# The first MLP product in twenty block products per quad, summed in two PSUM banks in five phases

## The chip, the cores and the metric

The kernel runs on one core of a Trainium2 chip. Times are device microseconds of one execution. Three runs of the kernel before took 558.06, 559.64 and 561.53 us; their median, 559.64 us, is the time before.

## The reference

A gated linear attention feeds a two-layer MLP with an ELU between. Inputs of the attention are q, k, v and f_logit with shape (4, 8, 768, 48): batch, heads, tokens, head dimension. w_in is 384 x 2048, w_out 2048 x 384.

```python
f = 1.0 / (1.0 + np.exp(-f_logit))
for t in range(S):
    state = f[:, :, t, :, None] * state + np.einsum('bhd,bhe->bhde', k[:, :, t], v[:, :, t])
    y[:, :, t] = np.einsum('bhd,bhde->bhe', q[:, :, t], state)
x = y.transpose(0, 2, 1, 3).reshape(3072, 384)
h = x @ w_in
g = np.where(h > 0.0, h, np.exp(np.minimum(h, 0.0)) - 1.0)
out = g @ w_out
```

Everything is fp32 in effect. The weights come as 64-bit floats; the kernel splits their words into fp32 itself, in a staging tile `area`, parts of which later hold sums of weight blocks.

## The kernel before

The 3072 tokens are cut into 12 **units** of 256 tokens (u or m = 0 to 11, three to a batch). Of each unit the attention gives x, held in tile `xt` as 128-row blocks: three blocks of rows (the 384 features) by two blocks of 128 tokens. The MLP of a unit runs over eight **pairs** j, each of 256 columns of w_in (two 128-column blocks). Below, p0 to p7 are a unit's pairs. For a pair the work is, in order:

1. *First product* (`up`, `up7`): x times the pair's columns into PSUM tiles `psH`. In units 1 to 11 it isn't done as 12 block products but as 11, with a bilinear scheme: `mix` forms four sums of weight blocks once for each pair, `blend` five differences of x blocks for each unit (on GpSimd), ten instructions (nine 128 wide, one 256 wide) multiply, and `u1`, `hh`, `u43h` on ScalarE and VectorE recombine the results to h (L911, L913, L926).
2. *Exponential* (`exped`): two ScalarE instructions, Relu of -h and Exp, into tile `gg` (L936, L937).
3. *ELU* (`elu`): one VectorE instruction forms g (L958), then four GpSimd instructions form the `sums` of g's blocks (L968).
4. *Second product* (`down`): seven products 192 wide into four PSUM tiles `psM` (L1015). The first and second read g alone, the third reads the third GpSimd sum. At a unit's end five VectorE adds join the four banks (L1025) and DMAs store the rows.

The order is written by hand, and every engine works through its own queue in that order. The main loop counts half-steps T, two to a pair: at even T the first product of pair P = T // 2 is issued, at odd T `joined(P)` and the second product of pair P - 2. A table `plan` puts attention work of later units at half-steps: `gates` (two ScalarE instructions on f, L617, L619), `decays` (a scan and a reciprocal on VectorE, scalings on GpSimd), `transposed`, `both` (state products, scores, the causal mask on VectorE at L722, the state updates at L695), `outputs` and `carried`, whose result ScalarE copies into `xt` (L779, L781); two SyncE DMAs (L784) then fill the gap rows of x, and `blend` may start. `reread` and `check` test the range of the weights, two VectorE reductions each.

The two PSUM banks of the first product have one tag, `h`, with two buffers: each pair takes both in turn. An instruction that waits on ScalarE, VectorE or GpSimd holds back all that stands behind it in that engine's queue.

## Time and profile before

| what | value |
|---|---|
| median of three runs | 559.64 us |
| span of the profiled execution | 557.7 us |
| TensorE (PE) busy | 543.0 us, 97% |
| VectorE (DVE) busy | 406.4 us, 73% |
| GpSimd (POOL) busy | 287.8 us, 52% |
| ScalarE (ACT) busy | 228.3 us, 41% |
| granted TensorE clock, mean | 0.994 |
| first product, 128 wide (PE, L904) | 1584 records in two groups |
| second product (PE, L1015) | 1236 records in four groups |

The page gives the profiled execution's span, from its first to its last instruction; no other time of that execution is listed, so sums are made against 557.7 us. A row of instruction groups has line, engine, operation, tiles out<-in, shapes and count, then the busy time and the mean of one in ns, then the engine's idle time before them and what ended it. An fp32 matrix product of one instruction appears as two records. Records on TensorE overlap, so the mean of one is its latency, not its share of the time. A timeline row has start, duration, engine, line and operation. A row of the chain of waits has start, duration and what ran.

### The profile page before, as it was taken

What the parts mean: (1) busy time and instruction counts of PE and PEld (TensorE: products, weight loads), DVE (VectorE), ACT (ScalarE), POOL (GpSimd) and SP (SyncE); (2) the same over time, 40 slices, a digit from 0 to 9 for tenths busy, and PEclk for the clock granted to TensorE, in tenths of its full rate; (3) what the DMA queues carried; (4) which work ended last, traced back from release to release, by engine and by line L of the source; (5) the groups of instructions that cost most, each with busy time, mean ns of one, the idle gap of its engine ahead of it and who ended that gap; (6) DMA issues with size and microseconds to landing.
All of it is one profiled execution on the core that took longest, in us unless ns stands there. A gap on an engine that the chain in (4) does not pass through costs nothing.

```text
span 557.7 us, 15617 instructions
## 1 busy us (share of the span) xinstructions
PE 543.0 (97%) x6358; PEld 507.9 (91%) x6358; DVE 406.4 (73%) x804; ACT 228.3 (41%) x443; POOL 287.8 (52%) x559
## 2 busy tenths in 40 slices
PE   7889999999999999999999999999999999999996
PEld 3477679999999999999999999999999999999996
DVE  8799888887676776786785785786686687745553
ACT  3279764333434343333434334343343344333331
POOL 6600786475473474375465366357258258325332
PEclk9899999999999999999999999999999999999998
DMA  8998971033035135216217207307307302301001
GB/s 211 261 264 214 278 184 43 4 84 88 3 82 146 30 76 149 63 34 186 68 22 186 81 9 192 87 8 192 86 9 191 88 9 72 88 5 33 31 2 35
DMA packets 39474, 54.30 MB, mean 97 GB/s; under 512 B 4032, under 2 KB 29216, under 8 KB 39392
## 3 DMA queue, kind: packets, MB, share of 16 engines
q1 hardware_dynamic: 38592, 52.61, 36.5%
q8 instruction: 52, 0.85, 0.6%
q10 hardware_dynamic: 800, 0.59, 0.4%
q14 instruction: 30, 0.25, 0.2%
HBM read 45.02 MB, written 4.72 MB: 89 GB/s over the span
## 4 chain that ended last, share of the span: by engine, by line
PE 91%; DMA 2%; DVE 2%; ACT 1%; POOL 1%; issue 1%; SPq 1%; ACTq 0%; DVEq 0%; POOLq 0%
PE psH L904 39%; PE psM L1015 37%; PE psM L981 3%; PE psH L949 2%; PE psY L752 2%; PE psY L772 2%; PE psU_a L737 2%; PE psS L714 2%; PE psT L674 1%; DMA area<-in_moe_w_out_dram 1%; DMA f<-f 1%; ACT area L578 1%; DVE f L636 1%; POOL q L626 1%; DMA f<-in_f_logit_dram 0%
## 5 line engine op out<-in xcount | busy, mean ns | idle before, releaser
L904 PE MATMUL psH<-xt,wi 128*128 128x128 f32 (+1 forms) x1056 | 195.0, 294 | 0.0
L968 POOL TENSOR_TENSOR sums<-gg 128x128 f32<-128x128 f32 x172 | 75.6, 460 | 207.8 <-DVE gg L958 188.1
L936 ACT ACTIVATE gg<-hh 128x512 f32<-128x512 f32 x88 | 55.5, 630 | 249.3 <-DVE hh L926 111.7
L904 PEld LDWEIGHTS psH<-xt,wi 128*128 128x128 f32 x1056 | 149.5, 192 | 1.6
L904 PE MATMUL psH<-xt,area 128*128 128x128 f32 x704 | 121.5, 275 | 0.0
L904 PEld LDWEIGHTS psH<-xt,area 128*128 128x128 f32 x704 | 106.5, 192 | 4.5
L913 DVE TENSOR_TENSOR hh<-psH,u 128x256 f32<-128x256 f32 x88 | 36.9, 419 | 97.8 <-ACT u L911 97.7
L1015 PE MATMUL psM<-area,sums 128*128 128x192 f32 x516 | 99.9, 326 | 0.0
L1015 PEld LDWEIGHTS psM<-area,sums 128*128 128x128 f32 x516 | 86.0, 190 | 0.3 <-issue 0.2
L1015 PE MATMUL psM<-wo,gg 128*128 128x192 f32 x376 | 77.7, 332 | 0.0
L958 DVE SCALAR_TENSOR_TENSOR gg<-gg,hh 128x512 f32<-128x512 f32 x88 | 63.8, 725 | 1.5 <-ACT gg L937 1.5
L636 DVE RECIPROCAL f<-f 128x256 f32<-128x256 f32 x36 | 62.7, 1747 | 1.3
L937 ACT ACTIVATE gg<-gg 128x512 f32<-128x512 f32 x96 | 60.6, 631 | 3.0
L1015 PEld LDWEIGHTS psM<-wo,gg 128*128 128x128 f32 x376 | 60.2, 190 | 1.3
L926 DVE TENSOR_TENSOR hh<-psH,u43h 128x256 f32<-128x256 f32 (+1 forms) x176 | 54.6, 352 | 3.0
L626 POOL TENSOR_TENSOR q<-q,f 128x256 f32<-128x256 f32 x48 | 39.6, 826 | 19.5 <-DMA f<-f 12.9
L968 POOL TENSOR_TENSOR sums<-gg,sums 128x128 f32<-128x128 f32 x86 | 45.4, 528 | 6.7
L626 POOL TENSOR_TENSOR k<-k,f 128x256 f32<-128x256 f32 x48 | 39.3, 821 | 10.2 <-DMA f<-f 8.3
L926 DVE TENSOR_TENSOR u43h<-psH,hh 128x256 f32<-128x256 f32 x88 | 37.0, 420 | 9.2 <-PE psH L904 8.7
L968 POOL TENSOR_TENSOR sums<-sums,gg 128x128 f32<-128x128 f32 x86 | 43.0, 500 | 0.0
L1015 PE MATMUL psM<-area,gg 128*128 128x192 f32 x172 | 42.0, 326 | 0.0
L1015 PE MATMUL psM<-wo,sums 128*128 128x192 f32 x172 | 42.0, 326 | 0.0
(102 smaller groups left out, 646.3 us busy)
## 6 DMA issues: line engine op xcount, KB each, us to landing
area<-in_moe_w_out_dram SPq DMA_DIRECT2D x8, 768.0 KB, 10.6
again<-in_moe_w_in_dram SPq DMA_DIRECT2D x16, 384.0 KB, 3.6
again<-in_moe_w_out_dram SPq DMA_DIRECT2D x16, 384.0 KB, 3.6
k<-in_k_dram SPq DMA_DIRECT2D x12, 384.0 KB, 4.5
q<-in_q_dram SPq DMA_DIRECT2D x12, 384.0 KB, 5.6
v<-in_v_dram SPq DMA_DIRECT2D x12, 384.0 KB, 5.8
area<-in_moe_w_in_dram SPq DMA_DIRECT2D x8, 576.0 KB, 8.3
out_dram<-o SPq DMA_DIRECT2D x42, 96.0 KB, 2.4
```

The source lines that it names most:

```text
L626: e.tensor_tensor(out=t[n][:, p], in0=t[n][:, p], in1=t["f"][:, p, "kq".index(n)], op=ALU.mult)
L636: nc.vector.reciprocal(f[:, p, 1], f[:, p, 0])
L714: nc.tensor.matmul(pc[r][FULL[b], w, p], lhsT=t["k"][FULL[r], p, cols], rhs=t["q"][FULL[r], p, cols], start=True, stop=True,)
L904: nc.tensor.matmul(to, lhsT=lhs, rhs=rhs, start=(n == 0), stop=True, skip_group_check=True)
L913: add = lambda to, x, y: nc.vector.tensor_tensor(out=to, in0=x, in1=y, op=ALU.add)
L926: add = lambda to, x, y: nc.vector.tensor_tensor(out=to, in0=x, in1=y, op=ALU.add)
L936: nc.scalar.activation(g[:], h, AF.Relu, scale=-1.0)
L937: nc.scalar.activation(g[:], g[:], AF.Exp, scale=-1.0)
L958: nc.vector.scalar_tensor_tensor(out=g[:], in0=g[:], scalar=-1.0, in1=phs.pop(P), op0=ALU.add, op1=ALU.max)
L968: nc.gpsimd.tensor_tensor(out=s[:, i], in0=x, in1=y, op=op)
L981: nc.tensor.matmul(pm[t][:], lhsT=g[:, i, t * 128 : (t + 1) * 128], rhs=wo[:, 2 * j + i, :], start=(j == 0 and i == 0), stop=(j == NP - 1 ...
L1015: nc.tensor.matmul(pm[bank][:, half * DH : (half + 1) * DH], lhsT=x, rhs=y, start=first, stop=(j == NP - 1), skip_group_check=True,)
```

## The change

Units 0 and 1 now do their first product plainly: `up` with six instructions, 256 wide, for a pair. From unit 2 on the eight pairs are taken as four **quads** of 512 columns (q0 to q3; quad n has pairs 2n and 2n + 1). A quad's 24 block products become 20, all 128 wide. For this 19 sums of weight blocks are formed once for each two quads in one instruction (`w_sums`, some of them in place of w_in's own blocks, which only the plain units needed), and 12 differences of x blocks for each unit (`blend`; `xt` now has 16 blocks and two buffers).

The 20 products are issued in five **phases** of 3, 5, 5, 4 and 3 (`phase`). Phases 0, 2 and 4 write one PSUM bank, 1 and 3 the other; later phases add to what the bank holds, and after each phase ScalarE copies the running sums to a tile `vals` in SBUF, so that each partial sum is caught on its way. After phase 1 ScalarE also writes one block back to PSUM (`SEED`). After phase 3 four VectorE instructions, after phase 4 three more (`JOIN3`, `JOIN4`, both operands in SBUF) complete h in `vals`.

The main loop from unit 2 on counts steps s, ten to a unit, each with two phases. In a step stand: the `elu` due, the plan's work, two phases with their copies and joins, more of the plan's work, then a number of second products from one running stream (`CHUNKS`: 6, 6, 6, 0, 7, 6, 6, 6, 7, 6), and at the end the exponential steps due: of a quad's first pair in the step where its phase 4 ran, of its second pair in the next. The elu of a pair stands at the start of the following step. The attention steps move with it: A3 places `transposed` in step 1, `both` in step 3, `outputs` in step 5, `carried` in step 6, BL `blend` in step 7; `gates` for the unit after next stands in step 5, its `decays` in steps 5, 7 and 8.

```diff
-    A3 = (2, 5, 9, 11)
-    BL = 13
-    MX = 10
+    D4 = (-9, -6, -4, -1)
+    A3 = (3, 7, 11, 13)
+    BL = 15
-    BL1 = 13
     LIMIT = 2.0**80
...
+        (10, 2, 0, -1), (7, 8, 14, -1), (2, 13, 5, -1), (11, 10, 9, -1), (15, 0, 14, -1), (6, 4, 15, -1),
+    )
...
+        (18, 17, 5, -1), (19, 18, 11, -1), (20, 9, 16, 1), (18, 18, 4, -1), (9, 15, 9, -1), (6, 10, 9, -1),
+        (8, 13, 3, -1), (0, 4, 8, -1), (5, 9, 12, -1), (3, 8, 12, -1), (12, 4, 19, -1), (4, 16, 11, -1),
...
+    PHASES = (
+        (0, 3, 0, 3, ((0, 15, 16), (1, 14, 13), (2, 13, 12))),
+        (1, 14, 0, 4, ((0, 5, 4), (3, 3, 6), (1, 5, 14), (1, 1, 7), (2, 0, 15))),
+        (0, 6, 0, 4, ((0, 12, 20), (1, 7, 8), (2, 4, 18), (3, 10, 1), (3, 4, 2))),
+        (1, 10, 0, 4, ((0, 2, 19), (3, 1, 5), (1, 8, 0), (2, 11, 9))),
+        (0, 0, 1, 3, ((1, 6, 17), (2, 9, 11), (3, 10, 3))),
+    )
+    SEED = (1, 5)
...
+    JOIN4 = (
...
+    PLACES = ((14, ((1, 1), (1, 0), (0, 0), (0, 1))), (4, ((1, 1), (0, 1), (1, 0), (0, 0))))
+    USUAL = ((0, 0), (0, 1), (1, 0), (1, 1))
...
+    def w_block(q, n):
+        if n >= 12:
+            return extra[:, q, n - 12]
+        i, k = divmod(n, NKT)
+        i = (0, 2, 3, 1)[i]
+        return wis[:, q, i // 2, k, i % 2]
+
+    def w_sums(e, q, some):
+        for to, a, b, sign in W_SUMS[some]:
+            e.tensor_tensor(
+                out=w_block(q, to), in0=w_block(q, a), in1=w_block(q, b), op=ALU.add if sign > 0 else ALU.subtract
+            )
 
     order = [divmod(i, NP) for i in range(NU * NP)]
...
+    def x_tile(u):
+        xts[u] = sb.tile([128, 16, 128], FP32, tag="xt", name=f"xt{u}", bufs=2)
+        return xts[u][:, 0:8].rearrange("n (k t) f -> n k (t f)", t=2)
+
...
-    def mix(j):
-
-        a = [[wi[j][:, k, i * 128 : (i + 1) * 128] for k in range(2)] for i in range(2)]
-        t = [mixes[:, j, i] for i in range(4)]
-        for to, x, y, op in (
-            (t[0], a[1][0], a[1][1], ALU.add), (t[1], t[0], a[0][0], ALU.subtract),
-            (t[2], a[0][0], a[1][0], ALU.subtract), (t[3], a[0][1], t[1], ALU.subtract),
-        ):
...
-    def blend(u):
-
-
-        x = xts[u][:].rearrange("n k (t i) -> n (k t) i", t=2)
-        for to, a, b in ((7, 3, 1), (1, 1, 0), (8, 3, 1), (9, 2, 8), (6, 4, 5)):
-            nc.gpsimd.tensor_tensor(out=x[:, to], in0=x[:, a], in1=x[:, b], op=ALU.subtract)
-
...
+    def blend(u, e, some=slice(None)):
+
+        x = xts[u]
+        for to, a, b, _ in X_SUMS[some]:
+            e.tensor_tensor(out=x[:, to], in0=x[:, a], in1=x[:, b], op=ALU.subtract)
+
+    quads = {}
+
+    def joins(n, todo):
+        v = vals[n % 2]
+        pick = lambda a, b: v[:, a : b + 1 : b - a] if b > a else v[:, a : a + 1].broadcast_to([128, 2, 128])
+        for op, to, x, y in todo:
+            nc.vector.tensor_tensor(out=pick(*to), in0=pick(*x), in1=pick(*y), op=op)
+
+    def phase(n, i):
+
+        m, q = PLAIN_UP + n // NQ, n % NQ
+        side, at, frm, size, todo = PHASES[i]
+        if i < 2:
+            quads[n, side] = ps.tile([128, 4, 128], FP32, tag=f"h{(n + side) % 2}", name=f"psH{m}_{q}_{side}")
+        bank = quads[n, side]
+        for t, (slot, x, w) in enumerate(todo):
+            nc.tensor.matmul(
+                bank[:, slot], lhsT=w_block(q, w), rhs=xts[m][:, x], start=(i < 2 and t == 0), stop=True,
+                skip_group_check=True,
+            )
+        v = vals[n % 2]
+        nc.scalar.copy(v[:, at : at + size], bank[:, frm : frm + size])
+        if i == 1:
...
-    def joined(P):
-        m, j = order[P]
-        h, pb = phs[P]
-        add = lambda to, x, y: nc.vector.tensor_tensor(out=to, in0=x, in1=y, op=ALU.add)
-        u43 = sb.tile([128, 2, 128], FP32, tag="u43h", name=f"u43h{m}_{j}")
-        add(u43[:], pb[:, 0::2], h[:, 0:1].broadcast_to([128, 2, 128]))
-        add(h[:, 2:4], pb[:, 1::2], u43[:])
-        add(h[:, 4], pb[:, 0], u43[:, 1])
-        exped(P, h[:, 1:].rearrange("n (i t) f -> n i (t f)", i=2))
-
...
-        if m >= DIRECT:
-            up7(P)
-            return
...
@@ -1009,9 +1041,11 @@
                 todo = todo[3:] + todo[:3]
             starts = ((0, 0), (3, 0), (1, 0), (2, 1)) if j == 0 else ((0, 0), (1, 0)) if j == plain else ()
         started = set()
-        for bank, half, x, y in todo:
+        for n, (bank, half, x, y) in enumerate(todo):
             first = (bank, half) in starts and bank not in started
             started.add(bank)
+            if n:
+                yield
             nc.tensor.matmul(
                 pm[bank][:, half * DH : (half + 1) * DH], lhsT=x, rhs=y,
...
+    for n in range(EARLY):
+        at_step(12 + n, lambda n=n: w_sums(nc.gpsimd, slice(0, 2), slice(n, n + 1)))
+        at_step(22 + n, lambda n=n: w_sums(nc.vector, slice(2, 4), slice(n, n + 1)))
+    for n in range(EARLY, len(W_SUMS)):
+        at_step(26 + (n - EARLY) // 2, lambda n=n: w_sums(nc.vector, slice(0, 2), slice(n, n + 1)))
+        at_step(32 + n - EARLY, lambda n=n: w_sums(nc.gpsimd, slice(2, 4), slice(n, n + 1)))
+    at_step(BL2, lambda: blend(2, nc.vector, slice(0, 6)), lambda: blend(2, nc.gpsimd, slice(6, 12)))
     for u in range(3, NU):
-        t = (u - 1) * NFT
-        at_step(t + BL, lambda u=u: blend(u))
-        at_step(t - 16, lambda u=u: load(u))
-        at_step(t - 8, lambda u=u: gates(u))
-        attention(u, [t + i for i in D3], [t + i for i in A3])
-    joint = [(u - 1) * NFT + A3[1] for u in range(3, NU)]
+        t = base(u - 1)
+        at_step(t + BL, lambda u=u: blend(u, nc.gpsimd))
+        at_step(base(u - 2), lambda u=u: load(u))
+        at_step(t - (8 if u == 3 else 10), lambda u=u: gates(u))
+        attention(u, [t + i for i in (D3 if u == 3 else D4)], [t + i for i in A3])
...
+    for T in range(PLAIN_UP * NFT):
         P = T // 2
...
+    def products():
+        for P in range(PLAIN_UP * NP - LAG, NU * NP):
+            for _ in down(P):
+                yield
+            yield
+
...
+    CHUNKS = (6, 6, 6, 0, 7, 6, 6, 6, 7, 6)
+
+    def exp_pair(n, i):
+        frm, where = PLACES[i]
+        exped(PLAIN_UP * NP + 2 * n + i, vals[n % 2][:, frm : frm + 4], where)
...
+    elu(PLAIN_UP * NP - 1)
+    total = (NU - PLAIN_UP) * NQ
+    for s in range(5 * total // 2):
+        T = PLAIN_UP * NFT + 2 * s
+        for f in elus.pop(s, ()):
+            f()
+        for f in plan.pop(T, ()):
+            f()
+        for i in (2 * s, 2 * s + 1):
+            n, i = divmod(i, 5)
+            phase(n, i)
+            if i == 3:
+                joins(n, JOIN3)
+            elif i == 4:
+                joins(n, JOIN4)
+                for z in range(2):
+                    exps.setdefault(s + z, []).append((n, z))
+        for f in plan.pop(T + 1, ()):
+            f()
+        take((5, 5, 4)[s] if s < 3 else CHUNKS[s % 10])
+        for n, z in exps.pop(s, ()):
+            exp_pair(n, z)
+            elus.setdefault(s + 1, []).append(lambda n=n, z=z: elu(PLAIN_UP * NP + 2 * n + z))
...
+    take(NP * 7)
```

Names in the next rows: `sums7_4` and `gg7_4` belong to unit 7, pair 4; `xt8` is x of unit 8. GpSimd in the second half of unit 7, before:

```order
L626 TENSOR_TENSOR k1_73<-k1_73,f1_71 128x256
L626 TENSOR_TENSOR q1_72<-q1_72,f1_71 128x256
L968 TENSOR_TENSOR sums7_5_4327<-gg7_5_4264 128x128 x2
L968 TENSOR_TENSOR sums7_5_4327<-sums7_5_4327,gg7_5_4264 128x128
L968 TENSOR_TENSOR sums7_5_4327<-gg7_5_4264,sums7_5_4327 128x128
L892 TENSOR_TENSOR xt8_4299<-xt8_4299 128x128 x5
L626 TENSOR_TENSOR k1_73<-k1_73,f1_71 128x256
L626 TENSOR_TENSOR q1_72<-q1_72,f1_71 128x256
L968 TENSOR_TENSOR sums7_6_4378<-gg7_6_4342 128x128 x2
```

and after:

```order
L1000 TENSOR_TENSOR sums7_3_4032<-gg7_3_4028,sums7_3_4032 128x128
L680 TENSOR_TENSOR k1_73<-k1_73,f1_71 128x256
L680 TENSOR_TENSOR q1_72<-q1_72,f1_71 128x256
L939 TENSOR_TENSOR xt8_4086<-xt8_4086 128x128 x12
L1000 TENSOR_TENSOR sums7_4_4136<-gg7_4_4132 128x128 x2
L1000 TENSOR_TENSOR sums7_4_4136<-sums7_4_4136,gg7_4_4132 128x128
L1000 TENSOR_TENSOR sums7_4_4136<-gg7_4_4132,sums7_4_4136 128x128
L680 TENSOR_TENSOR k1_73<-k1_73,f1_71 128x256
```

The subtractions for x went from five, behind the sums of p5 and ahead of those of p6, to twelve, ahead of the sums of p4. TensorE after, at the place that reads those sums (between `carried` and here stand 6 second products, 6 first, 6 second, 10 first and then the second products below):

```order
L957 MATMUL psH7_3_0_4109<-xt7_3586,area_134 128x128
L957 MATMUL psH7_3_0_4109<-xt7_3586,wi_132 128x128 x2
L1049 MATMUL psM7_1_3947<-area_134,sums7_3_4032 128x192
L1049 MATMUL psM7_2_3948<-area_134,gg7_3_4028 128x192
L1049 MATMUL psM7_2_3948<-wo_133,sums7_3_4032 128x192
L1049 MATMUL psM7_0_3946<-wo_133,gg7_4_4132 128x192
L1049 MATMUL psM7_3_3949<-wo_133,gg7_4_4132 128x192
L1049 MATMUL psM7_0_3946<-area_134,sums7_4_4136 128x192
```

The last row is the third product of p4; 17 second products and 16 first ones stand between `carried` and it. ScalarE in the middle of unit 7, before, with the gates (`f1`) and `u1` of p4:

```order
L936 ACTIVATE gg7_3_4136<-hh7_3_4118 128x512
L937 ACTIVATE gg7_3_4136<-gg7_3_4136 128x512
L617 ACTIVATE f1_71<-f1_71 128x3x256
L619 ACTIVATE f1_71<-f1_71 128x3x256
L911 COPY u1_7_4_4165<-psH7_4_0_4159 128x128
L936 ACTIVATE gg7_4_4185<-hh7_4_4167 128x512
```

and after, where `psH7_2_0` and `psH7_2_1` are the two banks of unit 7's third quad, q2:

```order
L970 ACTIVATE gg7_2_3957<-vals1_129 128x512
L971 ACTIVATE gg7_2_3957<-gg7_2_3957 128x512
L671 ACTIVATE f1_71<-f1_71 128x3x256
L673 ACTIVATE f1_71<-f1_71 128x3x256
L962 COPY vals0_128<-psH7_2_0_3968 128x384
L962 COPY vals0_128<-psH7_2_1_3973 128x512
L964 COPY psH7_2_1_3973<-vals0_128 128x128
L813 COPY between_131<-psY8_0_3981 128x8
```

The gates now stand between the exponential of p2 and the phase copies of q2; before, one copy of a recombination stood behind them. VectorE after, in steps 3 to 5 of unit 7 (`at8` is the masked scores, `vals1` the quad q1):

```order
L776 TENSOR_TENSOR at8_3879<-psS8_0_3880,twice_111 128x512
L776 TENSOR_TENSOR at8_3879<-psS8_1_3881,twice_111 128x512
L749 TENSOR_TENSOR state2_120<-psU8_a0_3845,state1_119 128x4x48
L749 TENSOR_TENSOR state3_121<-psU8_a1_3846,state2_120 128x4x48
L749 TENSOR_TENSOR state4_122<-psU8_a0_3845,state3_121 128x4x48
L990 SCALAR_TENSOR_TENSOR gg7_1_3921<-gg7_1_3921,vals0_128 128x512
L947 TENSOR_TENSOR vals1_129<-vals1_129 128x2x128 x7
L990 SCALAR_TENSOR_TENSOR gg7_2_3957<-gg7_2_3957,vals1_129 128x512
```

and before, at the same attention work:

```order
L926 TENSOR_TENSOR hh7_2_4011<-psH7_2_1_4004,u43h7_2_4025 128x128
L722 TENSOR_TENSOR at8_4066<-psS8_0_4067,twice_111 128x512
L722 TENSOR_TENSOR at8_4066<-psS8_1_4068,twice_111 128x512
L695 TENSOR_TENSOR state2_120<-psU8_a0_4032,state1_119 128x4x48
L695 TENSOR_TENSOR state3_121<-psU8_a1_4033,state2_120 128x4x48
L695 TENSOR_TENSOR state4_122<-psU8_a0_4032,state3_121 128x4x48
L608 TENSOR_REDUCE spans_145<-again16_3952 128x1 x2
L913 TENSOR_TENSOR hh7_3_4118<-psH7_3_0_4110,u1_7_3_4116 128x256
```

The mask and the state updates of unit 8 now stand ahead of an elu and all seven joins of a quad; before, they stood behind the joins of their pair and ahead of those of the next.

## The prediction

> **What bounds the kernel now.** I read the page first, then two windows, then the chain of waits, then TensorE's groups with shapes kept apart.

> ```profile
> span 557.7 us, 15617 instructions
> PE 543.0 (97%) x6358; PEld 507.9 (91%) x6358; DVE 406.4 (73%) x804; ACT 228.3 (41%) x443; POOL 287.8 (52%) x559
> 62.00:545.00 483.00, 482.95 (x5611) 465.63 (x5603) 348.77 (x718) 191.40 (x401) 261.38 (x499) 1.00 0.31 80
> 388.36:431.54 43.18, 43.18 (x520) 42.18 (x519) 31.91 (x67) 16.85 (x37) 23.39 (x46) 1.00 0.36 93
> 65.02 2.59 PE psH L949 x12
> ...
> 385.39 2.44 PE psH L904 x20
> 387.83 2.28 PE psM L1015 x14
> ...
> 428.57 2.44 PE psH L904 x20
> L904 PE MATMUL psH<-xt,wi 128*128 128x128 f32 x880 | 156.8, 276 | 0.0
> L904 PE MATMUL psH<-xt,wi 128*128 128x256 f32 x176 | 52.6, 380 | 0.0
> ```

> From 62 to 545 us TensorE is busy for 482.95 of 483.00 us at a granted clock of 1.00: it never waits there, so time is the sum of its products. (Columns of the window rows: PE, PEld, DVE, ACT, POOL.) The same place recurs after 428.57 - 385.39 = 43.18 us: one unit of 256 tokens. Each fp32 product leaves two records. A pair's first product is 2.44 us (9 products 128 wide, one 256 wide), its second 2.28 us (7 products, 0.326 each). The two shapes' mean times differ by 380 - 276 = 104 ns a record, so 20a + 2 x 0.104 = 2.44 gives a = 0.112: 0.223 us for a 128-wide product, 0.431 us for a 256-wide one. Attention has 43.18 - 8 x (2.44 + 2.28) = 5.42 us of each unit.

> **TensorE's own sum.** Before, a unit's first product is 8 x 2.44 = 19.52 us. After, it is 4 quads x 20 x 0.223 = 17.84: 1.68 us less, in ten units 16.8. Unit 1 goes plain: 8 pairs at 2.59 (the row at 65.02) = 20.7 for 19.5, 1.2 more, and its recombinations go. Net -15.6 us. The new period without a wait is 41.5 us.

> No other engine fills. ScalarE gains five copies and a seed per quad and loses two small copies:

> ```profile
> L827 ACT COPY xt<-psY 128x384 f32<-128x384 f32 x1 | 0.5, 480 | 1.8 <-PE psY L817 1.8
> L779 ACT COPY xt<-psY 128x512 f32<-128x512 f32 x11 | 6.4, 581 | 1.2 <-PE psY L772 1.2
> L911 ACT COPY u<-psH 128x128 f32<-128x128 f32 x88 | 23.1, 262 | 36.1 <-PE psH L904 36.0
> L892 POOL TENSOR_TENSOR xt<-xt x55: 452/457/1050, 72.1 to 506.4; 128x128 f32<-128x128 f32 x55
> 344.68 0.42 DVE L926 TENSOR_TENSOR u43h<-psH,hh 128x256 f32<-128x256 f32 x1 [0.23 <-PE psH L904]
> 345.13 0.62 DVE L926 TENSOR_TENSOR hh<-psH,u43h 128x256 f32<-128x256 f32 x2
> ```

> 4 x (2 x 0.48 + 3 x 0.58 + 0.26) - 8 x 0.26 = +9.8 us on 16.85. GpSimd gets seven more additions for x, 7 x 0.457 = +3.2 us on 23.4. VectorE's seven joins per quad, a dependent one starting 0.45 us after the last (345.13 - 344.68), replace eight adds; about nothing. Engines are served in order, though, so I walked their queues from one event to the next. Three chains in each unit come out longer than the TensorE work that covers them. "p4" is the unit's fifth pair, "q2" its third quad.

> **Wait C: GpSimd's twelve additions in front of p4's sums.**

> ```profile
> 366.95 1.16 PE L772 MATMUL psY<-q,state 64*64 64x64 f32 x64
> 369.44 0.57 ACT L779 COPY xt<-psY 128x512 f32<-128x512 f32 x1
> 370.03 1.18 ACT L781 COPY xt<-psY 64x512 f32<-64x512 f32 x2
> xt<-xt SPq DMA_DIRECT2D x20, 48.0 KB, 2.2
> 375.02 2.48 POOL L892 TENSOR_TENSOR xt<-xt 128x128 f32<-128x128 f32 x5
> 379.28 0.87 POOL L968 TENSOR_TENSOR sums<-gg 128x128 f32<-128x128 f32 x2
> 380.11 0.46 POOL L968 TENSOR_TENSOR sums<-sums,gg 128x128 f32<-128x128 f32 x1
> ```

> The count starts where `carried` ends on TensorE. Before, the three copies waited 1.3 us for ScalarE; in the new queue only phase copies stand ahead, 0.3. Copies 1.77 (369.44 to 371.21), the gap DMA 2.2: 4.3 us. Then twelve additions at 2.48/5: 5.95. Then p4's first three sums, since the third product of p4 reads the third: 380.57 - 379.28 = 1.29. With four handovers of some 0.06 us that is 11.8 us. TensorE has until then 16 first products and 17 second ones, 16 x 0.223 + 17 x 0.326 = 9.1. The wait is 2.7. In the old order the five additions stood behind a pair's sums and nothing on TensorE was late. Low end: no copy waits and 12 x 0.457: 1.8. High end: copies 0.7 late, additions at 0.53 (the page's mean for the third sum is 528 ns), sums 1.5: 4.0. I take 3.0, near the chain as measured with a little for collisions. Nine units (2 to 10) have it: 27 us.

> **Wait B: the gates and a phase copy behind q1's joins.**

> ```profile
> 350.25 1.14 PE L714 MATMUL psS<-q,k 64*64 64x64 f32 x64
> 351.56 1.28 DVE L722 TENSOR_TENSOR at<-psS,twice 128x512 f32<-128x512 f32 x2
> 352.75 1.13 DVE L695 TENSOR_TENSOR state<-psU_a,state 128x192 f32<-128x192 f32 x3
> 358.01 0.83 ACT L617 ACTIVATE f<-f 128x768 f32<-128x768 f32 x1
> 358.87 0.84 ACT L619 ACTIVATE f<-f 128x768 f32<-128x768 f32 x1
> 360.95 1.16 PE L752 MATMUL psY<-at,v 64*64 64x64 f32 x64
> 546.88 0.63 ACT L936 ACTIVATE gg<-hh 128x512 f32<-128x512 f32 x1 [2.46 <-DVE hh L926]
> 547.55 0.63 ACT L937 ACTIVATE gg<-gg 128x512 f32<-128x512 f32 x1
> 548.27 0.69 DVE L958 SCALAR_TENSOR_TENSOR gg<-gg,hh 128x512 f32<-128x512 f32 x1 [1.48 <-ACT gg L937]
> ```

> From the scores' end: masks done after 1.45, four state updates (3 take 1.13) 2.9, p1's elu 3.6, q1's seven joins 7 x 0.45 = 6.7. VectorE held the joins behind all this; ScalarE, waiting for them, holds the gates (358.01 to 359.71, 1.70) and the copy of q2's first phase behind p2's two exponential steps (546.88 to 548.18, 1.30): 8.1, 9.8, and the copy 10.4. q2's third phase may not add to that bank before. TensorE's cover: 15 first and 13 second products and `outputs`, 3.35 + 4.24 + 1.25 = 8.8. The wait is 1.6; 1.1 with one state update fewer and joins at 0.42, 2.6 if GpSimd's sums for p1 slow the joins by a third of a microsecond each way. I take 1.8, eight times (unit 10 has no gates): 14 us.

> **Wait A: p6's elu.** From the end of q3's fourth phase: copy 0.2 + 0.58, joins 3.15, exponentials 0.1 + 1.30, elu 0.1 + 0.69, handover 0.1: 6.2 us, against 11 first and 10 second products, 2.45 + 3.26 = 5.7. I take 0.5 (0.2 to 0.9), nine times: 4.5 us.

> **The ends.** After the last phase the same chain has only ten second products over it, 3.3 of 5.55, and then p6's third sum is late by 0.75: 3.0 us (2 to 4) where the old end has no idle time on TensorE:

> ```profile
> 545.51 0.82 PE L1015 MATMUL psM<-wo,gg 128*128 128x192 f32 x4
> ...
> 552.01 0.49 PE L1015 MATMUL psM<-wo,sums 128*128 128x192 f32 x2
> ```

> (21 products in 6.85 us.) In unit 1 VectorE loses eight recombinations of about 1.5 us and gains 19 weight sums and six for x, crowded into the last ten half-steps; GpSimd's 32 weight sums become 19 of twice the width, nine of them in unit 2. No row shows that crowd: 0 to 4 us, I take 1.5.

> **Sum**: 557.7 - 15.6 + 27 + 14.4 + 4.5 + 3.0 + 1.5 = 592.5 us. The page gives the profiled execution only its span; the median of the runs, 559.64, is 1.9 more: 594.4, rounded to 595. The low ends (16.2 + 8.8 + 1.8 + 2 + 0) give 573, the high ends (36 + 20.8 + 8.1 + 4 + 4) 617.

> [...] The joins now read two SBUF operands. In the trace the one step that did so, the elu, has a mean of 725 ns against 680 when one operand lay in PSUM, so such reads aren't cheaper here:

> ```profile
> L958 DVE SCALAR_TENSOR_TENSOR gg<-gg,hh 128x512 f32<-128x512 f32 x88 | 63.8, 725 | 1.5 <-ACT gg L937 1.5
> L958 DVE SCALAR_TENSOR_TENSOR gg<-gg,psH 128x512 f32<-128x512 f32 x8 | 5.4, 680 | 0.2 <-ACT gg L937 0.2
> ```

> [...]

> **Rivals.**
> *1. Faster: the three chains fit.* TensorE's saving of 15.6 us is certain. It shows if C is covered: the twelve additions and the three sums would have to end 2.7 us sooner, at 0.27 us an addition where no row is under 0.452. Or the sum of the three waits stays under 1.1 us a unit for another reason, a copy or DMA that starts earlier than I walked it. For it: GpSimd is only half busy. Against: no row shows such an addition. 557.7 - 15.6 + 3 + 1.9 = 547. Chance 0.12. The waits decide from (15.6 - 4.5)/9 = 1.2 us a unit on: over it the kernel is slower.
> *2. C alone,* A and B hidden by work I left out: 557.7 - 15.6 + 27 + 3 + 1.9 = 574, or at C's low end 563. The first is slower, chance 0.12; the second within 1%, 0.07.
> *3. Collisions in full.* GpSimd's additions have a median of 457 ns and one of 1050, the elu a mean 45 ns over its least: VectorE and GpSimd hinder each other when both read SBUF. If each join and the addition beside it wait for one another whole, 0.46 us, C grows by 3 x 0.42 and B and A by 1.8 (four joins): 9 x 1.3 + 8 x 1.8 + 9 x 0.9 = 34 more, 629; half of it 612. Chance of over 617: 0.08. [...]
> *4. The clock.* Idle stretches of about 3 us, nine times, could lower the granted clock. Against: the idle before 30.28 us passed without a slow product behind it.

> ```profile
> 30.28 0.92 PE L949 MATMUL psH<-xt,wi 128*128 128x256 f32 x3 [1.67 <-DVE xt L829]
> ```

> That was 1.67 us, though, shorter than C. If 3.4 us of work ran at half rate after each C: 9 x 3.4 = 31 more, 626. Chance 0.03. [...]

> **How the numbers follow.** The forecast with its bounds (573 to 617) has 0.58. Within 1% of 559.6, about what a measurement tells from no change, lies only rival 2's low end: 0.07. Faster by more: 0.12. Slower: 0.58 + 0.12 + 0.08 + 0.03 = 0.81. The range has to hold 0.8: from 560, which takes in C alone and half of its low end, to 620, leaving out rival 1 whole, and most of 3 and 4.

> **What would show it.** TensorE in a middle unit would have a period near 47 us of which some 42 are busy; the waits view would list TensorE waiting for GpSimd's sums (about 3 us, third product of p4), for ScalarE's phase copy (q2, about 1.8), for VectorE's elu (p6, 0.5). A first product would stay at 0.112 us a record. The additions for x would start about 4.4 us after `carried` and take about 6. If TensorE stays above 99% busy from 90 us on, the walk of the queues was wrong; if it waits but at other places, the sum was right by accident.

## The result

The changed kernel takes 625.17 us (median of four runs, 624.01 to 628.21) against 559.41 for the kernel before in the same comparison: a ratio of 1.118, 95% interval 1.114 to 1.121. It is slower, as forecast, but by 66 us and not by 35; the range ended at 620. The profiled execution took 624.47 us with a span of 622.7, 65.0 us more than the span before.

The page after, its busy row and its clock row in 40 slices:

```profile
PE 554.0 (89%) x6294; PEld 510.2 (82%) x6294; DVE 442.0 (71%) x757; ACT 318.9 (51%) x595; POOL 326.4 (52%) x603
PEclk9999999989889989989979989999998997999998
```

The waits view after, for TensorE (us in total, times, longest):

```profile
PE psM L1049 <- POOL sums L1000: 28.0, 10, 4.4
PE psH L957 <- ACT vals L962: 11.0, 9, 1.7
PE psM L1049 <- DVE gg L990: 10.2, 15, 2.4
PE psH L957 <- DVE gg L990: 4.7, 2, 3.5
```

The waits are where the forecast put them: wait C for GpSimd's sums, B for a phase copy, A (and the tail) for an elu. TensorE's idle time went from 14.7 to 68.7 us. But its busy time went up as well, from 543.0 to 554.0, though it has less to do. The clock row shows one reason: most units have a slice below full speed, from a *slow stretch* of 3.41 or 6.83 us in which TensorE runs at half clock (granted 0.50, 368.97 to 372.38 us for one).

Windows from one wait C to the next, the first row a unit without a slow stretch, the second the sum and mean of seven units (columns PE, PEld, DVE, ACT, POOL):

```profile
418.03:466.85 48.82, 42.60 (x519) 40.81 (x519) 36.14 (x63) 26.16 (x53) 28.46 (x52) 1.00 0.32 82
...
sum 347.48, PE 309.77 PEld 297.84 DVE 248.75 ACT 181.52 POOL 195.61; mean PE 44.25 PEld 42.55 DVE 35.53 ACT 25.93 POOL 27.94
```

Six units of the kernel before, from the end of one `carried` to the next:

```profile
sum 258.72, PE 258.72 PEld 252.74 DVE 188.83 ACT 99.81 POOL 139.31; mean PE 43.12 PEld 42.12 DVE 31.47 ACT 16.64 POOL 23.22
```

A unit lasted 258.72 / 6 = 43.12 us and lasts 347.48 / 7 = 49.64 us. Of that TensorE is idle for 5.39, which is the forecast's sum of waits (3.0 + 1.8 + 0.5 = 5.3). What is over is its busy time: 44.25 where 41.5 was forecast. At first sight the clock, a rival given 0.03, is the missing term: 44.25 - 42.60 = 1.65 us a unit.

One unit's waits on TensorE's timeline (start, duration, what ran, and in brackets the idle time before it and what ended it):

```profile
414.32 0.92 PE L1049 MATMUL psM<-wo,gg 128*128 128x192 f32 x4 [0.19 <-DVE gg L990]
418.03 0.92 PE L1049 MATMUL psM<-area,sums 128*128 128x192 f32 x4 [2.80 <-POOL sums L1000]
427.53 0.76 PE L1049 MATMUL psM<-wo,gg 128*128 128x192 f32 x3 [1.96 <-DVE gg L990]
450.92 0.49 PE L957 MATMUL psH<-xt,area 128*128 128x128 f32 x2 [1.24 <-ACT vals L962]
```

C is 2.80 and B 1.24, but A in this unit, which ran at full clock, is 1.96 and not 0.5. In the seven units with a slow stretch behind C it is shorter, 0 to 1.61. So two explanations stood against each other. **The clock**: TensorE's time is its stream, the waits add to it, and the half-speed stretches are the term that was left out. **The loop**: the time from C to A is a chain over ScalarE and VectorE that doesn't depend on TensorE's clock, so a slow stretch there costs little, and what was mis-sized is that chain.

### The profile page after: what moved, and what is told of

Read it like the earlier page. It is cut to its first block, busy times and chain, and to the rows that moved or that the text cites. A ratio compares the mean times of both kernels' runs of the same rounds, so it can differ in the third digit from the quotient of the medians.

```text
span 622.7 us, 15560 instructions
## 1 busy us (share of the span) xinstructions
PE 554.0 (89%) x6294; PEld 510.2 (82%) x6294; DVE 442.0 (71%) x757; ACT 318.9 (51%) x595; POOL 326.4 (52%) x603
## 4 chain that ended last, share of the span: by engine, by line
PE 38%; DVE 26%; POOL 13%; ACT 10%; issue 6%; DMA 6%; SPq 1%; ACTq 0%; DVEq 0%; POOLq 0%
PE psM L1049 14%; PE psH L957 14%; DVE vals L947 13%; POOL xt L939 9%; PE psH L980 3%; DVE gg L990 3%; POOL sums L1000 3%; ACT gg L970 2%; DMA f<-f 2%; DVE f L690 2%; ACT vals L962 2%; DVE f L685 2%; ACT gg L971 2%; PE psS L768 1%; PE psU_a L791 1%
## 5 line engine op out<-in xcount | busy, mean ns | idle before, releaser
L1000 POOL TENSOR_TENSOR sums<-gg 128x128 f32<-128x128 f32 x172 | 83.3, 504 | 203.9 <-DVE gg L990 189.4
L947 DVE TENSOR_TENSOR vals<-vals 128x256 f32<-128x256 f32 x280 | 142.1, 519 | 67.0 <-ACT vals L962 59.2
L962 ACT COPY vals<-psH 128x512 f32<-128x512 f32 (+1 forms) x200 | 105.1, 540 | 122.7 <-PE psH L957 121.5
L957 PE MATMUL psH<-xt,wi 128*128 128x128 f32 x880 | 144.7, 286 | 3.5 <-DVE gg L990 3.5
L1049 PE MATMUL psM<-area,sums 128*128 128x192 f32 x516 | 112.5, 343 | 28.0 <-POOL sums L1000 28.0
L957 PEld LDWEIGHTS psH<-xt,wi 128*128 128x128 f32 x880 | 125.5, 202 | 3.7 <-DVE gg L990 3.7
L970 ACT ACTIVATE gg<-vals 128x512 f32<-128x512 f32 x80 | 50.4, 630 | 104.7 <-DVE vals L947 76.0
L990 DVE SCALAR_TENSOR_TENSOR gg<-gg,vals 128x512 f32<-128x512 f32 x80 | 58.2, 728 | 59.6 <-ACT gg L971 51.7
L1049 PE MATMUL psM<-wo,gg 128*128 128x192 f32 x376 | 80.5, 336 | 10.2 <-DVE gg L990 10.2
L939 POOL TENSOR_TENSOR xt<-xt 128x128 f32<-128x128 f32 x114 | 59.9, 553 | 9.2 <-DMA xt<-xt 3.9
L680 POOL TENSOR_TENSOR q<-q,f 128x256 f32<-128x256 f32 x48 | 39.0, 813 | 18.7 <-DMA f<-f 15.6
L980 PE MATMUL psH<-xt,wi 128*128 128x256 f32 x192 | 45.1, 384 | 2.3 <-DVE xt L887 1.7
```

What stands on the lines that cost most here:

```text
L680: e.tensor_tensor(out=t[n][:, p], in0=t[n][:, p], in1=t["f"][:, p, "kq".index(n)], op=ALU.mult)
L939: e.tensor_tensor(out=x[:, to], in0=x[:, a], in1=x[:, b], op=ALU.subtract)
L947: nc.vector.tensor_tensor(out=pick(*to), in0=pick(*x), in1=pick(*y), op=op)
L957: nc.tensor.matmul(bank[:, slot], lhsT=w_block(q, w), rhs=xts[m][:, x], start=(i < 2 and t == 0), stop=True, skip_group_check=True,)
L962: nc.scalar.copy(v[:, at : at + size], bank[:, frm : frm + size])
L970: nc.scalar.activation(g[:], h, AF.Relu, scale=-1.0)
```

## The experiments

### The clock alone

In wait C's place TensorE gets three products into a free bank (`warm`):

```diff
-        take((5, 5, 4)[s] if s < 3 else CHUNKS[s % 10])
+        if s % 10 == 8:
+            take(5)
+            warm(3, "a0")
+            take(2)
+        else:
+            take((5, 5, 4)[s] if s < 3 else CHUNKS[s % 10])
```

> Nothing is left out: three 128x512 products into a free bank (their result is not read) are issued on TensorE in the place where it stands in wait C, so that it works through the wait. The waiting itself does not end earlier. Theory (the half-clock windows come from C's idle time): the windows behind C go, the granted clock rises from 0.963 to 0.985 or more, and the time falls to 605, 600 to 612 us. Rival (the clock drops for another reason, such as the work's own density): clock within 0.005 of 0.963 and 623 to 635 us, the fill costing what it overhangs.

627.45 us (ratio 1.122, 1.119 to 1.124), clock 0.982 to 0.988 for 0.960 to 0.969. The page's busy row:

```profile
PE 568.6 (91%) x6354; PEld 509.1 (82%) x6354; DVE 444.0 (71%) x757; ACT 318.7 (51%) x595; POOL 328.2 (53%) x603
```

Two rows of its waits view, and of its seven units' windows one unit and the sum row:

```profile
PE psM L1049 <- DVE gg L990: 19.0, 16, 2.1
PE psM L1049 <- POOL sums L1000: 4.1, 9, 1.1
```

```profile
463.54:514.39 50.85, 46.83 (x540) 43.55 (x540) 36.18 (x64) 25.93 (x52) 28.40 (x52) 0.97 0.29 79
...
sum 345.80, PE 319.55 PEld 296.69 DVE 250.77 ACT 181.70 POOL 198.46; mean PE 45.65 PEld 42.38 DVE 35.82 ACT 25.96 POOL 28.35
```

Both expectations were half right. The slow stretches behind C do come from its idle time: filled, they are gone. Yet the time stayed: a unit takes 345.80 / 7 = 49.40 us. Much of what the clock gave back, wait A took, which is now 1.8 to 1.97 us in the first eight units, and the waits for an elu went from 10.2 to 19.0 us. From the end of C to the end of A pass 9.50 us in a unit at full clock (418.03 to 427.53), 10.2 on the mean of the changed kernel's first eight units, 9.45 here. So of 1.65 us a unit that the clock seems to cost, some 0.7 counted. Part of that was lost again: in two units of this run a slow stretch now follows A. The one shown takes 50.85 us, the five at full clock 48.98 on the mean.

### One wait's cause at a time

Gates earlier by three half-steps, for wait B:

```diff
-        at_step(t - (8 if u == 3 else 10), lambda u=u: gates(u))
+        at_step(t - (8 if u == 3 else 13), lambda u=u: gates(u))
```

> A unit's two ScalarE gate activations are issued three steps earlier in the unit before it (13 ahead instead of 10), so they no longer stand between two phase copies behind q1's joins. Theory (wait B is ScalarE's order): TensorE's waits on the phase copies, 10.8 us in eight places of the changed kernel's trace, go or fall under 2 us in all, wait C (27.0 us) and the windows at half clock stay; 625 less about 10, 612 to 618 us. Rival (the phase copy is late because the joins on VectorE are late, not because of the gates): the waits stay within 2 us of 10.8 and the time at 622 to 628.

619.99 us (1.108, 1.104 to 1.112). The waits on phase copies fell from 11.0 to 0.2 us, so B is ScalarE's order, as worked out. But the waits for an elu rose from 10.2 to 14.5, and the time fell by 5.2 us only, half of the waits; 612 to 618 was expected.

The x differences, for wait C:

```diff
-        at_step(t + BL, lambda u=u: blend(u, nc.gpsimd))
+        at_step(t + BL, lambda u=u: nc.gpsimd.memset(xts[u][:, 8:16], 0.0))
```

> Left out: GpSimd's 12 x differences of every unit from the fourth on; one GpSimd fill of x's blocks 8 to 15 stands in their place, so the output is not the reference's. Sum of waits (each wait is a term of its own): wait C's 27.0 us of the changed kernel go and nothing takes their place, and the half-clock windows behind them go: 625 - 27 - 20 = 578, 572 to 590 us. Loop (the unit's period is one chain around VectorE, ScalarE, GpSimd and TensorE, so a wait taken away at one place comes back in part at another, as the run with the fill on TensorE suggests, whose clock was 0.988 and whose time did not fall): 590 to 612 us, with wait A longer than the 6.3 us that it had.

593.66 us (1.061, 1.058 to 1.064), clock 0.995 in the profiled execution; a unit takes 45.93 us there. That is 31.5 less and in the range of the loop, 590 to 612; the sum of waits had 572 to 590. Two rows of the waits view:

```profile
PE psM L1049 <- DVE gg L990: 12.5, 10, 2.4
PE psM L1049 <- POOL sums L1000: 8.3, 16, 1.0
```

The span fell by 34.1: TensorE's busy time by 17.3 (554.0 to 536.7), as no slow stretch follows C any more, and its idle time by 16.8 only. The waits for sums kept 8.3 of their 28.0 us and those for an elu grew by 2.3 (10.2 to 12.5), which again is the loop. The joins didn't change (512 ns on the mean, 519 before).

The joins, for wait A:

```diff
-            nc.vector.tensor_tensor(out=pick(*to), in0=pick(*x), in1=pick(*y), op=op)
+            nc.vector.tensor_tensor(out=pick(*to)[:, :, 0:64], in0=pick(*x)[:, :, 0:64], in1=pick(*y)[:, :, 0:64], op=op)
```

> Left out: half the columns of each of VectorE's joins (280 instructions of 519 ns become about 300 ns, some 6 us a unit less on VectorE), so the output is not the reference's. Sum of waits: only wait A (6.3 us) ends at the joins, so 617 to 621 us. Loop: about 20% of the chain of a middle unit is joins, so the period falls by some 3 to 4.5 of its 49.5 us and the time to 585 to 598 us, with wait C shorter too, since the decays of the next unit stand behind joins on VectorE.

606.77 us (1.084, 1.079 to 1.089): 18.4 less, though wait C stayed (28.3 us for all waits for sums). It lies between the two ranges, 585 to 598 and 617 to 621. The sum of waits has no place for so much; of the loop's figure a part is missing because half the columns took 385 ns and not some 300. The waits for an elu and those for a phase copy both became shorter (10.2 to 4.2 and 11.0 to 4.4 us).

All three together:

> The last two edits together with the gates three steps earlier: fill in place of the x differences, joins of half the columns, gates at 13 ahead; work left out as in those, no product among it. It shows what TensorE's stream alone takes: if the forecast's term for TensorE (15.6 us less than before) is right and no other wait stands behind A, B and C, the time is 558 - 15.6 and some 8 us of waits at the second unit's start and at the tail, 545 to 556 us. If the 20 products and four phases a quad cost TensorE more than was worked out, or another wait comes up, 560 or more.

564.12 us (1.008, 1.006 to 1.010). The sum row of seven units, and two rows of its waits view:

```profile
sum 298.98, PE 292.97 PEld 286.47 DVE 220.61 ACT 181.78 POOL 152.30; mean PE 41.85 PEld 40.92 DVE 31.52 ACT 25.97 POOL 21.76
```

```profile
PE psM L1049 <- DVE gg L990: 8.1, 9, 1.4
PE psH L957 <- DVE gg L990: 4.6, 2, 3.5
```

Here TensorE's stream is seen almost bare: 41.85 us a unit where 41.5 was forecast and 43.12 were needed before. The saving is real, 1.3 us a unit. But even with a quarter of the joins' time (388 ns for 519) and all of the differences' taken away the kernel only draws near the old one, outside what was expected (545 to 556).

The three single gains are 5.2 + 31.5 + 18.4 = 55.1 us, together 61.1: with these three cut, 61 of the 66 us come back.

The part of the change in the second unit, alone in the kernel before:

```diff
-        if m >= DIRECT:
+        if m >= 2:
...
-    at_step(BL1, lambda: blend(1))
...
```

> The kernel before with one part of the change alone: the second unit's first product plain (no x differences and no joins for it). By the forecast 1.2 us longer, 560 to 562 us; if the second unit was held by VectorE before, no change or up to 3 us less.

559.70 against 559.17 us (1.001, 0.999 to 1.003). No difference that can be measured; the 1.2 us of the forecast lie inside the interval.

### Moving steps, with no work left out

Gates earlier and second products later:

```diff
-    CHUNKS = (6, 6, 6, 0, 7, 6, 6, 6, 7, 6)
+    CHUNKS = (9, 9, 9, 0, 7, 6, 6, 3, 4, 3)
```

> The gates three steps earlier and the number of second products per step changed from 6,6,6,0,7,6,6,6,7,6 to 9,9,9,0,7,6,6,3,4,3, so that the second products of the pair whose sums stand behind the x differences come after the next unit's first phases. No work is added or left out. Theory (waits A, B and C are all order, and the clock follows C): 6.3 + 10.8 + 27.0 us of waits mostly go and with them about 20 us of clock; 625 - 60 = 565, 556 to 578 us. Rival (GpSimd and VectorE work bounds the unit: VectorE was busy some 41 of 49 us): the wait comes back elsewhere, on the joins or the x differences, and the time stays over 590.

608.12 us (1.087, 1.083 to 1.091). A went and the waits for sums fell to 9.2 us, but TensorE now waits 15.3 us for phase copies and 10.0 for the block that ScalarE writes back to PSUM, because few products are left to cover them. The rival had it: the wait comes back elsewhere.

Seven of the 12 differences on VectorE, and the gates earlier:

```diff
-        at_step(t + BL, lambda u=u: blend(u, nc.gpsimd))
+        at_step(t + BL, lambda u=u: blend(u, nc.gpsimd, (0, 1, 2, 10, 11)))
+        at_step(t + BL, lambda u=u: blend(u, nc.vector, (3, 5, 6, 4, 8, 7, 9)))
```

> No work is added or left out: seven of a unit's 12 x differences move from GpSimd (0.55 us each) to VectorE (0.26 us each in the second unit's), where it stands idle for 1.5 us behind the joins, and the gates come three steps earlier. Loop (a unit's period is TensorE's stream plus the gaps that the chains over the other engines leave, and of the half-clock time only some 0.7 us a unit counts): wait C from 2.8 to 0.7, the clock back above 0.985, wait B gone, wait A up to 1.1 to 2; the period from 49.6 to 45.5 to 46.5 us and the time to 588 to 598 us. Sum of waits with the whole of the half-clock time counted: 625 - 10 - 19 - 20 = 576. Rival (VectorE takes the loss, since joins and decays stand behind the differences there): 605 or more.

597.29 us (1.066, 1.064 to 1.069), in the range of the loop: C is 0.75, the waits for an elu now 22.0 us. On VectorE a difference took 0.28 to 0.29 us in its trace with GpSimd idle, but two of the seven some 0.54 beside a GpSimd instruction, 0.37 on the mean. Then second products two and, in the next kernel, four later, and, on the first of these, the start of the third unit put right:

```diff
-    CHUNKS = (6, 6, 6, 0, 7, 6, 6, 6, 7, 6)
+    CHUNKS = (7, 7, 6, 0, 7, 6, 6, 4, 7, 6)
...
+    CHUNKS = (7, 7, 8, 0, 7, 6, 6, 4, 6, 5)
...
+        if T == PLAIN_UP * NFT - 1:
+            elu(PLAIN_UP * NP - 1)
         for f in plan.pop(T, ()):
...
-        at_step(22 + n, lambda n=n: w_sums(nc.vector, slice(2, 4), slice(n, n + 1)))
+        at_step(22 + n, lambda n=n: w_sums(nc.vector if n > 5 else nc.gpsimd, slice(2, 4), slice(n, n + 1)))
```

> The run before, and the second products of a unit's last steps come two products later (7,7,6,0,7,6,6,4,7,6 for 6,6,6,0,7,6,6,6,7,6). Loop: C gone, A under 1; period 44 to 45, 574 to 584 us. Rival (the gap moves to the phase copies, as in the run with 9,9,9): no faster than the run before.

> As the run before, but up to four products later (7,7,8,0,7,6,6,4,6,5): A gone as well; period 43 to 44, 566 to 578 us if no other wait comes; with the rival of the run before 580 or more.

> The second of these four with the start of the third unit put right: the last elu of the plain units is issued one step earlier and six of the w_in sums go from VectorE to GpSimd. The wait there (3.5 of the 4.7 us at two places) falls under 1.5 us: 3 to 4 us less than that run.

602.69, 601.76 and 597.20 us (1.077, 1.075 and 1.068). The first two are slower than the kernel before them, as their rival had it. In the first C is gone and A is 2.2 to 2.4 us in the first eight units; in the second A is gone and a wait of 2.5 us for a phase copy stands in its place. The third gained 5.5 us over the first where 3 to 4 were expected; the wait at the third unit's start fell from 4.6 to 2.5, over the 1.5 forecast. So far every gap that was closed opened another, and A's chain was the tightest part of the ring.

### Why A's chain is long

The seven joins ahead of wait A in the changed kernel on VectorE's timeline, and what GpSimd did beside them:

```profile
420.50 4.82 DVE L947 TENSOR_TENSOR vals<-vals 128x256 f32<-128x256 f32 x7 [1.97 <-ACT vals L962]
```

```profile
420.17 1.07 POOL L1000 TENSOR_TENSOR sums<-gg 128x128 f32<-128x128 f32 x2
421.20 0.64 POOL L1000 TENSOR_TENSOR sums<-sums,gg 128x128 f32<-128x128 f32 x1
421.91 0.52 POOL L1000 TENSOR_TENSOR sums<-gg,sums 128x128 f32<-128x128 f32 x1
422.39 0.91 POOL L680 TENSOR_TENSOR q<-q,f 128x256 f32<-128x256 f32 x1
423.26 0.91 POOL L680 TENSOR_TENSOR k<-k,f 128x256 f32<-128x256 f32 x1
424.13 0.91 POOL L680 TENSOR_TENSOR q<-q,f 128x256 f32<-128x256 f32 x1
```

The forecast had 7 x 0.45 = 3.15 us here; they took 4.82. The view by tile of the first four and the last three (min/median/max in ns):

```profile
L947 DVE TENSOR_TENSOR vals<-vals x4: 425/561/561, 420.5 to 422.1; 128x256 f32<-128x256 f32 x4
L947 DVE TENSOR_TENSOR vals<-vals x3: 768/831/944, 422.8 to 424.4; 128x256 f32<-128x256 f32 x3
```

Beside 128-wide sums a join takes 561 ns, beside the 256-wide scalings of q and k 768 to 944. Over the whole trace 110 joins with GpSimd idle take 423 ns on the mean, 79 with GpSimd busy all through 608.

The same trace holds the counterpart. For unit 10 there is no unit after next, so no scalings, and GpSimd's sums end before the joins begin:

```profile
566.68 3.13 DVE L947 TENSOR_TENSOR vals<-vals 128x256 f32<-128x256 f32 x7 [4.07 <-ACT vals L962]
572.03 0.92 PE L1049 MATMUL psM<-wo,gg 128*128 128x192 f32 x4 [0.30 <-DVE gg L990]
```

There the joins take 3.13 us and A is 0.30, as the forecast has them, and C's end to A's end takes 7.8 us (564.22 to 572.03, full clock). With the disturbed joins alone it was 9.5 (the unit at full clock above); with a slow stretch alone it is 9.3, in the same unit of the run with earlier gates (557.47 to 566.75); with both it is 9.6 to 10.7. Alone the joins add 1.7 us and the slow stretch 1.5, together 2.5 on the mean of seven units: in part they hide each other.

The test moves the three scalings behind p6's sums, in the kernel of 597.20 us:

```diff
-    D4 = (-9, -6, -4, -1)
-    A3 = (3, 7, 11, 13)
+    D4 = (-9, -6, -4, 1)
+    A3 = (5, 7, 11, 13)
```

> The run before (second products two later, third unit's start put right) with one more move: GpSimd's three 256-wide scalings of q and k (0.7 to 0.9 us each), which there run beside the seven joins ahead of wait A, come two half-steps later, behind p6's sums, and the transposes that need them one step later. Collision theory (a join takes 423 ns with GpSimd idle and 608 beside it in the changed kernel's trace, so the seven joins ahead of A take 4.5 to 4.8 us where the forecast had 3.15): the seven joins fall to 3.9 or less, wait A from 2.2 to 1.2 us or less, the time from 597 to 585 to 591 us. Rival (the joins are as slow for another reason, such as their operands both lying in SBUF): seven joins stay at 4.4 or more, A over 2, 595 to 600 us.

580.23 us (1.037, 1.034 to 1.040): 17.0 us less than without the move, more than expected. The joins and six units of the kernel without the move, then the same of the one with it:

```profile
355.16 4.54 DVE L947 TENSOR_TENSOR vals<-vals 128x256 f32<-128x256 f32 x7
sum 279.90, PE 259.37 PEld 250.09 DVE 226.88 ACT 154.81 POOL 148.80; mean PE 43.23 PEld 41.68 DVE 37.81 ACT 25.80 POOL 24.80
```

```profile
345.71 3.60 DVE L947 TENSOR_TENSOR vals<-vals 128x256 f32<-128x256 f32 x7
sum 269.38, PE 254.60 PEld 245.31 DVE 224.54 ACT 153.59 POOL 151.88; mean PE 42.43 PEld 40.89 DVE 37.42 ACT 25.60 POOL 25.31
```

The joins are 0.94 us shorter and wait A fell by the same, from 2.23 to 1.29 us; the operands still both lie in SBUF, so that alone wasn't the reason. A unit went from 46.65 to 44.90 us: 0.94 from A, and 0.80 of TensorE's busy time, because behind a shorter A no slow stretch follows any more (clock 0.976 to 0.993). There the clock counted in full: in the kernel without the move, units with a slow stretch behind A take 1.4 to 1.7 us longer than like units without one (47.43 for 45.78).

### Is the rest order or capacity?

Four kernels change that of 580.23 us further. The first puts the exponential steps of an odd quad's first pair behind the next step's phase copies, with second products up to four later. The second and the fourth are the first with other places for the decays, and the third is the second with products up to six later:

```diff
-                    exps.setdefault(s + z, []).append((n, z))
+                    exps.setdefault(s + max(z, n % 2), []).append((n, z))
...
+    CHUNKS = (7, 7, 8, 0, 7, 6, 6, 4, 6, 5)
...
-    D4 = (-9, -6, -4, 1)
+    D4 = (-9, -4, -3, 1)
...
+    CHUNKS = (7, 8, 9, 0, 7, 6, 6, 3, 5, 5)
...
+    D4 = (-9, -4, 0, 1)
```

> The run before (580) with two moves: ScalarE's exponential steps of an odd quad's first pair come behind the next step's phase copies instead of ahead of them, and second products come up to four later (7,7,8,0,7,6,6,4,6,5). Order theory (everything above TensorE's 42 us a unit is waiting that the queues' order makes, and wait A can be covered now that the joins before it take 3.6 us): wait A (1.3 us and some 0.3 beside it, nine times) goes and no wait on a phase copy takes its place; 580 - 14 = 566, 563 to 571 us. Capacity theory (VectorE is too busy to be covered, a gap moves only): 576 or more.

> The run above, and of the next unit's decays (a scan and a reciprocal on VectorE, 2.5 us) the second stands behind p4's elu instead of ahead of p4's joins, the third one half-step later. Order theory: TensorE's wait for p4's elu (0.8 to 1.3 us, nine times) goes as well; 556 to 564 us. Capacity theory: as before, 572 or more.

> The run above with second products up to six later (7,8,9,0,7,6,6,3,5,5). Order theory: no wait left in a middle unit, period 42 to 42.6 us, 550 to 558 us; if buffers bind or a wait on phase copies comes in, 560 to 570.

> The first of these four with the second decays behind p4's elu and the third ones behind p6's. Order theory: wait A and p4's wait both gone, 553 to 562 us; if the third decay now holds p7's elu or the transposes, 560 to 570.

584.23, 599.54, 592.23 and 615.49 us (1.046, 1.070, 1.060 and 1.101). None gained, and all lie above the ranges of the order theory. A row of the waits view of the first of them, and the same row of the last:

```profile
PE psM L1049 <- POOL sums L1000: 11.3, 10, 1.3
```

```profile
PE psM L1049 <- POOL sums L1000: 33.0, 9, 4.7
```

Before these moves this wait stood at 1.0 us. In the last, p6's sums stand behind scalings in GpSimd's queue that wait for the moved decays and a DMA of `f` behind them. These orders fell, all four. That doesn't show that an engine is full: VectorE is busy for 37.4 of 44.9 us in the best kernel. Whether some order of the change beats the kernel before stays open; none that ran did, and the best, at 580.23 us, is 3.7% slower.

## Why the prediction was wrong

The direction was right, and so were the three waits and their causes; the size was 30 us short (624.47 for 594.4). By its steps:

- *TensorE's own sum*, 41.5 us a unit: right within 0.4, by the run with the causes of all three waits cut (41.85). The second unit's 1.2 us couldn't be told from nothing.
- *Wait C*, 3.0: right, 2.57 to 4.44 with six of nine near 2.8, 27.0 in all. Two errors cancel in it: the additions took 553 ns and not 496, so the chain 12.56 us and not 11.8, but what TensorE did meanwhile took 9.76 and not 9.1 (the unit of 418.03).
- *Wait B*, 1.8, eight times: 0.85 to 1.67, 10.8 us in all for 14.4. That the gates ahead of the copy cause it is shown by the run that moved them.
- *Wait A*, 0.5: this is the step that failed. "Joins 3.15" took 4.82 us, since GpSimd's sums and the scalings of a later unit run beside them. At full clock A is 1.96: from the copy's start (419.88) to TensorE's next product (427.53) pass 7.65 us, and by the forecast 6.0. Where nothing of GpSimd stood beside the joins, they took 3.13 and A was 0.30. Rival 3 had this mechanism, but as a case of its own with 0.08, with a collision at four of the seven joins and half of its price for A; the term of the sum should have had it, because the walk of the queues showed what GpSimd does at that moment.
- *The clock*, rival 4: it came, after seven of the nine waits C and at three more places, and TensorE's records grow by 1.65 us a unit. A chance of 0.03 was too small: the trace of the kernel before has such a stretch too, 18.93 to 22.35 us at a granted 0.50, behind a window of the same length in which TensorE was busy for 1.50 us. But behind C a slow stretch covers much of what A would have waited anyway, so some 0.7 of the 1.65 counted, and filling C made the kernel no faster. 31 us for it on top of the sum would have hit the total (626) for a wrong reason.
- *The ends*: the tail's two waits are 2.37 + 0.99 us for 3.0. The third unit's start is out of its bounds: VectorE's weight sums stand ahead of the last plain elu, 1.15 + 3.50 = 4.65 us for 1.5 (0 to 4).

A unit is 49.64 - 46.8 = 2.84 us longer than forecast (46.8 is 41.5 and the three waits), nine times 25.6 us. Of the 2.84 some 2.4 lie between the end of C and the end of A, where the joins and the clock act: by the forecast's prices 15 first and 12 second products and A are 7.26 + 0.5 = 7.8 us, and 10.2 were measured. Another 3.1 us come at the third unit's start; a little over 1 us of the 30 is left unexplained. That the idle time came out as forecast (5.39 for 5.3) is an accident: A is 0.88 on the mean of the seven units, and 1.96 where no slow stretch covers it.

The signs told which was which: C, B and A lay where they should, the additions for x started 4.6 us after the copies behind `carried` began (405.51 to 410.11) and took 6.63, but the period was 49.6 and not 47, and A stood at four times its size in the one unit that had a full clock and disturbed joins.

*Where the operands lie.* The forecast put the elu's 725 ns for 680 down to where its operands lie. The view by tile of the kernel before (min/median/max in ns) says otherwise:

```profile
L958 DVE SCALAR_TENSOR_TENSOR gg<-gg,hh x88: 674/681/1212, 83.9 to 548.3; 128x512 f32<-128x512 f32 x88
L958 DVE SCALAR_TENSOR_TENSOR gg<-gg,psH x8: 673/678/689, 35.7 to 74.1; 128x512 f32<-128x512 f32 x8
```

The medians are alike; the mean hid two groups. Of the 88 with both operands in SBUF, 65 ran with GpSimd idle and took 681 ns on the mean, 23 beside a GpSimd instruction, 850. The 128x256 adds with one operand in PSUM took 415 to 420 either way. So the old trace could have shown what happens to a join.

Joins with GpSimd idle take 423 ns, and the adds of the same shape with one operand in PSUM took 419 and 420 before: on its own, a join that reads SBUF alone was neither shorter nor longer. What lengthened it ran beside it: the joins of 768 to 944 ns beside scalings of 910 (some 720 with VectorE idle), the seven joins' fall from 4.54 to 3.60 us when the scalings moved, and the elu's two groups, 681 and 850 ns, all show this.

## What to carry to other kernels

A chain that crosses engines has to be priced with what the other engines do at that moment: the same join took 423 ns alone and up to 944 beside a long GpSimd instruction. A mean can hide this: split an instruction's rows by what ran beside them. In a ring of queues a wait taken away comes back in part at the next tight place, so the size of a wait isn't what its removal gains (10.8 us of wait B gave 5.2; work cut on the joins gave 18.4 where A was 6.3); find the tightest chain and shorten its work. A lower clock cost in full where TensorE was what others waited for (1.4 to 1.7 us a unit behind A), and some 0.7 of 1.65 us behind C, where others were late anyway: before counting slow records, see whether a wait behind them becomes shorter.

## What the runs showed of the hardware

```profile
365.55:368.97 3.42, 0.62 (x4) 0.33 (x3) 3.38 (x5) 1.02 (x2) 3.26 (x8) 1.00 0.03 6
368.97:372.38 3.41, 3.41 (x16) 3.41 (x16) 0.25 (x1) 0.45 (x1) 3.33 (x7) 0.50 0.96 240
...
413.34:416.75 3.41, 1.70 (x9) 1.11 (x7) 3.21 (x3) 2.50 (x6) 3.33 (x7) 1.00 0.00 0
416.75:420.17 3.42, 2.14 (x17) 2.14 (x18) 1.77 (x4) 0.29 (x1) 3.34 (x7) 1.00 0.57 80
```

Both waits C are 2.80 us long. The first falls into one window, which is busy for 18%, and the next runs at half speed. The second straddles two, 50% and 63% busy, and nothing happens. In the traces of the kernel before and of the changed one (from 20 us on) all 9 full-speed windows that were busy for less than 44% were followed by half speed, none of 304 over 55%, and 2 of 6 between. A half-speed window that was busy for over 80% was followed by full speed (9 of 9), one below by another (4 of 4). So a wait of 2.80 us had half speed behind it in one place and not in the other, by where it fell; and two waits that lay in one window in part (1.98 us of the 2.37 and 0.51 of the 0.99 in the tail of the changed kernel, the window from 607.90, busy for 27%) had it behind them together.

The elu and the joins, with both operands in SBUF, took longer beside a GpSimd instruction (681 and 850 ns in the kernel before, 423 and 608 in the changed one); the adds of 128x256 with an operand in PSUM didn't (420 and 415, before). A difference of two 128x128 blocks took 0.55 us on the mean on GpSimd, and on VectorE 0.28 to 0.29 with GpSimd idle, both in the changed kernel.
